# Attention outputs of blocks 2 to 5: one group of TensorE instructions per block instead of two

## The chip, the cores and the metric

The kernel runs on one core of one Trainium2 chip. The metric is device time in microseconds (us) of one execution, lower is better. An execution takes about 234 us. The engines are called as the profile calls them: PE (TensorE matmul), PEld (its weight loads), DVE (VectorE), ACT (ScalarE), POOL (GpSimd), SP (SyncE).

## The reference, cut to what matters

```python
# q, k, v: batch 4, heads 8, sequence 768, head_dim 64; lam: one decay per head
for b in range(nb):                                   # blocks of the sequence
    intra = einsum('bhic,bhjc->bhij', qb, kb) * Dmask      # masked scores
    intra = einsum('bhij,bhjd->bhid', intra, vb)           # scores times v
    inter = einsum('bhid,bhde->bhie', qb * lam_pow, kv_state)   # state product
    out[:, :, sl] = intra + inter
    kv_state = lam_block * kv_state + einsum('bhsd,bhse->bhde', kb_dec, vb)
# x = out as [3072 tokens, 512]
gate = sigmoid(x @ w_gate); val = x @ w_val           # 512 -> 1536
y = (gate * val) @ w_out                              # 1536 -> 512
```

The reference uses blocks of 64 positions. The kernel uses blocks of 128, so six blocks, numbered 0 to 5. In the kernel a block covers 128 positions of all four batches, and its feed-forward part works on 512 tokens at a time.

## The kernel before

The kernel lists the instructions of each engine in an order fixed by hand. Feed-forward work of block n and attention work of block n+1 alternate in the PE stream. These pieces matter here:

```python
ps_at = tile_pool(name="ps_at", bufs=5, space=PSUM)   # scores, outputs, state updates
ps_ff = tile_pool(name="ps_ff", bufs=3, space=PSUM)   # gate, value, projection

def piece_a(n, bs):                    # attention outputs of the batches bs
    for b in bs:                       # state products: 128x128 weights
        OP[n, b] = ps_at.tile([128, HP, C], FP32, name="op", tag="ps")
        for hp in range(HP if n > 0 else 0):
            nc.tensor.matmul(OP[n, b][:, hp, :], lhsT=Sb[:, b, hp, :],
                             rhs=QS[n, b // 2][:, b % 2, hp, :],
                             start=(hp == 0), stop=False, ...)
    for b in bs:                       # score products: 128x64 weights, two column halves
        for hp in range(HP):
            for u in range(2):
                us = slice(u * 64, (u + 1) * 64)
                nc.tensor.matmul(OP[n, b][us, hp, :], lhsT=V[n][:, b, 2 * hp + u, :],
                                 rhs=MT[n, b][:, u, hp, :], ...)
    ...
    for b in bs:                       # output of the attention = input of the feed-forward
        nc.scalar.copy(XT[n][:, :, b, :], OP[n, b])

def a(n, bp):
    piece_a(n, [2 * bp, 2 * bp + 1])   # two batches

    # step n of the loop (n = 2 to 4); block 2 has the same tail, written out before the loop
    gv(n, 0)                           # gate and value matmuls, one slice of d_ff
    c(n, 0)                            # state update, batches 0 and 1
    ...
    sc(nx, 1); m(nx, 1)                # scores of the next block (PE), masked by DVE into MT
    piece_po(n, 1)                     # projection: 12 matmuls of 128x512
    a(nx, 0)
    piece_po(n, 2)
    a(nx, 1)
    piece_po(n, 3)
    # next step begins with gv(nx, 0), which reads XT[nx] of all four batches
```

Per batch the attention output takes 4 state products (full 128x128 weights) and 8 score products (weights of 64 columns, each writing one half of the PSUM partitions). So one group of two batches is 8 state products and 16 score products.

Of the kernel before, what the change touches and what calls it, by code (L numbers as in the profile page):

```python
# [16 lines left out]
def kernel(  # L17
# [13 lines left out]
    B, H, S, D = q.shape  # L31
# [39 lines left out]
    def load(n, what, b0, b1):  # L71
        sl = slice(n * C, (n + 1) * C)
        for c in what:
            lst, src = {"q": (Q, q), "k": (K, k), "v": (V, v)}[c]
            if n not in lst:
                lst[n] = qkv.tile([128, B, H, D], BF16, tag=c + "b", name=c + "b")
            t = lst[n]
            nc.gpsimd.dma_start(  # L78
                out=t[:, b0:b1],
                in_=src[b0:b1, :, sl, :].rearrange("b h s d -> s (b h) d"))  # L80
# [71 lines left out]
    def transpose_by_dma(n):  # L152
        QR[n] = trsb.tile([128, B, HP, C], BF16, tag="QR", name="QR", bufs=2)
        kt = trsb.tile([128, B, HP, C], BF16, tag="KR", name="KR", bufs=2)
        for dst, src in ((QR[n], Q[n]), (kt, K[n])):
            nc.sync.dma_start_transpose(out=dst.rearrange("p b g c -> p (b g) c"),
                                        in_=src.rearrange("p b h d -> p (b h d)"))
        for bp in range(2):
            KS[n, bp] = kt[:, 2 * bp:2 * bp + 2]
# [69 lines left out]
    def piece_a(n, bs):  # L229
        for b in bs:  # L230
# [4 lines that stand above are left out]
                                 start=(hp == 0), stop=False, skip_group_check=True)  # L235
        for b in bs:
# [4 lines that stand above are left out]
                                     rhs=MT[n, b][:, u, hp, :],  # L241
                                     start=(n == 0 and hp == 0), stop=(hp == HP - 1),
                                     skip_group_check=True)
        if n not in XT:
            XT[n] = xtp.tile([128, NMT, B, C], BF16, tag="XT", name="XT")
        for b in bs:
            nc.scalar.copy(XT[n][:, :, b, :], OP[n, b])  # L247
# [12 lines left out]
    def make_kd(n):  # L260
        KD[n] = kdp.tile([128, B, H, D], BF16, tag="kd", name="kd")
        nc.gpsimd.tensor_tensor(  # L262
            out=KD[n], in0=K[n],
            in1=kds.unsqueeze(1).unsqueeze(3).to_broadcast([128, B, H, D]), op=ALU.mult)
# [3 lines left out]
    def fade():  # L268
        for b in range(B):
            SD[b] = kdp.tile([128, HP, 128], FP32, tag="sd", name="sd", bufs=4)  # L270
            nc.gpsimd.tensor_tensor(out=SD[b], in0=Sb[:, b],  # L271
                                    in1=dec.unsqueeze(2).to_broadcast([128, HP, 128]),
                                    op=ALU.mult)
# [54 lines left out]
    def piece_last(n, tt):  # L328
        ob = osb.tile([128, DM], FP32, tag="ob", name="ob")
        for lo, hi in ((0, 384), (384, DM)):  # L330
            po = ps_ff.tile([128, DM], FP32, name="po", tag="ff")
            for ft in range(NFT):
                nc.tensor.matmul(po[:, lo:hi], lhsT=HT[n, ft][:, tt * 128:(tt + 1) * 128],  # L333
                                 rhs=WO[:, ft, lo:hi], start=(ft == 0), stop=(ft == NFT - 1))
            if lo == 0:
                nc.scalar.copy(ob[:, lo:hi], po[:, lo:hi])
            else:
                nc.vector.tensor_copy(ob[:, lo:hi], po[:, lo:hi])
            nc.sync.dma_start(out=out[tt * S + n * C:tt * S + (n + 1) * C, lo:hi], in_=ob[:, lo:hi])

    def piece_po(n, tt):
        po = ps_ff.tile([128, DM], FP32, name="po", tag="ff")
        for ft in range(NFT):
            nc.tensor.matmul(po, lhsT=HT[n, ft][:, tt * 128:(tt + 1) * 128],  # L344
                             rhs=WO[:, ft, :], start=(ft == 0), stop=(ft == NFT - 1))
        ob = osb.tile([128, DM], FP32, tag="ob", name="ob")
        nc.scalar.copy(ob, po)  # L347
        nc.sync.dma_start(out=out[tt * S + n * C:tt * S + (n + 1) * C, :], in_=ob)
# [45 lines left out]
    def c(n, bp):  # L394
        piece_c(n, [2 * bp, 2 * bp + 1])

    def t(n, bp):
        piece_t(n, bp)

    def sc(n, bp):  # L400
        piece_s(n, [2 * bp, 2 * bp + 1])
        piece_m(n, 2 * bp)

    def m(n, bp):
        piece_m(n, 2 * bp + 1)

    def a(n, bp):
        piece_a(n, [2 * bp, 2 * bp + 1])

    def gv(n, *fts):  # L410
        for ft in fts:
            piece_gv(n, ft)
# [48 lines left out]
    sc(2, 1)  # L461
    m(2, 1)
    piece_po(1, 1)
    a(2, 0)
    piece_po(1, 2)
    a(2, 1)
    piece_po(1, 3)
    for n in range(2, NSTEP):
        nx = n + 1
        if nx == NSTEP:  # L470
            gv(n, *range(NFT))
            for tt in range(B - 1):
                piece_po(n, tt)
            piece_last(n, B - 1)
            break
        transpose_by_dma(nx)
        gv(n, 0)
        c(n, 0)
        gv(n, 1)
        c(n, 1)  # L480
        if nx + 1 < NSTEP:
            fade()
            make_kd(nx)
            load(nx + 1, "qkv", 0, B)
        gv(n, 2, 3, 4, 5, 6, 7, 8)
        t(nx, 0)
        gv(n, 9)
        t(nx, 1)
        gv(n, 10)
        sc(nx, 0)  # L490
        gv(n, 11)
        m(nx, 0)
        piece_po(n, 0)
        sc(nx, 1)
        m(nx, 1)
        piece_po(n, 1)
        a(nx, 0)
        piece_po(n, 2)
        a(nx, 1)
        piece_po(n, 3)  # L500


# [28 lines left out]
```

## Time and profile before

| | before |
|---|---|
| time, median of 3 runs | 234.06 us (233.78 to 234.13) |
| span of the profiled run | 231.8 us |
| PE / DVE / ACT / POOL busy | 97% / 46% / 35% / 36% |
| share of PE in the chain that ended last | 91% |
| granted PE clock | full in every slice |

These are lines of the page of the kernel before: its head, the busy times, PE and its granted clock (in tenths, in 40 slices of the span), and the chain of work that ended last.

```profile
span 231.8 us, 3884 instructions
...
PE 224.9 (97%) x1566; PEld 116.1 (50%) x1566; DVE 106.3 (46%) x186; ACT 80.8 (35%) x147; POOL 84.4 (36%) x73
...
PE   7799999999999999999999999999999999999994
...
PEclk9999999999999999999999999999999999999999
...
PE 91%; POOL 6%; issue 1%; ACT 0%; DVE 0%; POOLq 0%
```

PE is the bottleneck, and after the first slices it has no rest. So what leaves the PE stream here should shorten the run, and what PE must wait for should lengthen it. Busy time itself will not show the change, because the ends of matmuls in the profile are modelled and overlap. What one reads is the distance from start to start.

The next lines are the PE instructions of block 4's attention outputs, from the timeline of the kernel before. The columns are start in us, length in us, engine, line, operation, output<-inputs, shape of the weights (rows*columns), and how many instructions are merged in the line.

```profile
154.25 0.61 PE L233 MATMUL op<-QS,Sb 128*128 128x128 bf16 x8
154.79 0.64 PE L240 MATMUL op<-MT,vb 128*64 128x128 bf16 x16
155.36 2.76 PE L344 MATMUL po<-WO,ht 128*128 128x512 bf16 x12
157.96 0.61 PE L233 MATMUL op<-QS,Sb 128*128 128x128 bf16 x8
158.50 0.64 PE L240 MATMUL op<-MT,vb 128*64 128x128 bf16 x16
159.07 2.76 PE L344 MATMUL po<-WO,ht 128*128 128x512 bf16 x12
161.67 0.59 PE L299 MATMUL gp<-XT,WG 128*128 128x512 bf16 x2
```

The shape changes where L233 ends and where L240 ends. From the start of the state products to the start of the score products it is 0.54 us, although eight of them at 56 ns would be 0.45. The score products take 0.57 us, where eight pairs at 56 ns would take 0.45. The single records show where the difference sits: 149 ns from the last state product to the first score product instead of 56; 77 ns to the second pair instead of 53; 152 ns from the last pair to the projection instead of 53; 226 ns after the projection's first matmul instead of 216. These four excesses, 93 + 24 + 99 + 10, add up to 226 ns for one group. From the projection to the state products, both with 128-column weights, it is 216 ns, which is the ordinary step.

### The profile page before, as it was taken

The page shows a single profiled execution, that of the slowest core. Times are in us where ns is not written, and L with a number is a line of the kernel's source. Part 1 is how long each engine was busy: PE and PEld are TensorE (multiplying, and loading weights), DVE is VectorE, ACT ScalarE, POOL GpSimd, SP SyncE. Part 2 cuts the span into 40 slices and gives each one's busy share as a digit, 9 for nine tenths or more (in the row PEclk, how much of TensorE's full clock was granted, in tenths as well). Part 3 has the DMA queues.
Part 4 walks back from the last instruction along what each step waited for, and adds up shares of the span by engine and source line. Part 5 has one row for each costly group of instructions (what it writes and reads, how often), then busy time and mean ns, then how long its engine had stood idle before and what let it go on. Part 6 is the DMA issues. An engine that isn't in the chain of part 4 may idle for free.

```text
span 231.8 us, 3884 instructions
## 1 busy us (share of the span) xinstructions
PE 224.9 (97%) x1566; PEld 116.1 (50%) x1566; DVE 106.3 (46%) x186; ACT 80.8 (35%) x147; POOL 84.4 (36%) x73
## 2 busy tenths in 40 slices
PE   7799999999999999999999999999999999999994
PEld 2444555788544455544455544455544455444442
DVE  4362757554870530845640845840754750243300
ACT  5653343554222224333134243233333223434221
POOL 8999988770596000695000596000000000000000
PEclk9999999999999999999999999999999999999999
DMA  8999999999949992919921919931820012100022
GB/s 57 144 177 174 162 192 158 198 183 156 138 88 120 206 217 75 166 36 134 138 93 45 189 42 113 154 90 53 184 47 0 0 45 93 45 0 0 3 90 91
DMA packets 102465, 24.89 MB, mean 107 GB/s; under 512 B 91568, under 2 KB 99504, under 8 KB 102448
## 3 DMA queue, kind: packets, MB, share of 16 engines
q0 software_dynamic: 82064, 14.16, 83.7%
q1 hardware_dynamic: 20384, 10.49, 20.1%
q8 instruction: 12, 0.20, 0.4%
q14 instruction: 5, 0.04, 0.0%
HBM read 28.32 MB, written 6.29 MB: 149 GB/s over the span
## 4 chain that ended last, share of the span: by engine, by line
PE 91%; POOL 6%; issue 1%; ACT 0%; DVE 0%; POOLq 0%
PE po L344 26%; PE gp L299 24%; PE vp L305 24%; PE vp L322 3%; PE op L240 3%; PE gp L316 3%; PE sp L210 2%; PE op L233 2%; PE cp L279 2%; POOL vb L78 1%; PE po L333 1%; POOL MT L222 1%; POOL qb L78 1%; POOL kb L78 1%; POOL WV L85 1%
## 5 line engine op out<-in xcount | busy, mean ns | idle before, releaser
L308 DVE TENSOR_TENSOR ht<-sg,vp 128x512 bf16<-128x512 bf16 x65 | 44.7, 688 | 85.7 <-PE vp L305 85.4
L305 PE MATMUL vp<-XT,WV 128*128 128x512 bf16 x260 | 66.7, 379 | 0.0
L299 PE MATMUL gp<-XT,WG 128*128 128x512 bf16 x260 | 66.8, 379 | 0.0
L302 ACT ACTIVATE sg<-gp 128x512 bf16<-128x512 f32 x65 | 38.8, 597 | 74.6 <-PE gp L299 74.5
L344 PE MATMUL po<-WO,ht 128*128 128x512 bf16 x276 | 62.6, 380 | 0.0
L344 PEld LDWEIGHTS <-ht 128*128 128x128 bf16 x276 | 25.9, 98 | 30.8
L305 PEld LDWEIGHTS <-WV 128*128 128x128 bf16 x260 | 25.4, 98 | 31.0 <-DMA WV<-in_moe_w_val_dram 0.5
L299 PEld LDWEIGHTS <-WG 128*128 128x128 bf16 x260 | 24.5, 98 | 27.4 <-DMA WG<-in_moe_w_gate_dram 0.4
L271 POOL TENSOR_TENSOR sd<-Sb,dec 128x512 f32<-128x512 bf16 x16 | 16.3, 1038 | 54.0 <-DVE Sb L288 54.0
L227 DVE TENSOR_TENSOR MT<-sp,mask 128x512 bf16<-128x512 f32 x44 | 27.8, 683 | 13.5 <-PE sp L210 13.5
L347 ACT COPY ob<-po 128x512 f32<-128x512 f32 x23 | 13.5, 586 | 52.5 <-PE po L344 48.7
L262 POOL TENSOR_TENSOR kd<-kb,kds 128x2048 bf16<-128x2048 bf16 x5 | 18.1, 3624 | 2.3 <-DMA kb<-in_k_dram 2.3
L247 ACT CAST XT<-op 128x512 bf16<-128x512 f32 x23 | 12.4, 588 | 5.0 <-PE op L240 5.0
L288 DVE TENSOR_TENSOR Sb<-cp,sd 64x256 bf16<-64x256 f32 x32 | 13.5, 420 | 0.8
L78 POOL DMA_DIRECT2D qb<-in_q_dram x9 | 12.4, 1385 | 0.8 <-POOLq L515 0.8
L78 POOL DMA_DIRECT2D vb<-in_v_dram x9 | 12.2, 1360 | 0.0
L78 POOL DMA_DIRECT2D kb<-in_k_dram x8 | 11.5, 1434 | 0.0
L145 PE MATMUL wm<-zero 128*128 128x512 bf16 x26 | 8.9, 477 | 1.2 <-DVE zero L97 1.2
L326 DVE TENSOR_TENSOR ht<-sg,vp 128x256 bf16<-128x256 bf16 x14 | 5.8, 420 | 6.2 <-PE vp L322 3.8
L322 PE MATMUL vp<-XT,WV 128*128 128x256 bf16 x56 | 8.4, 272 | 0.1
L316 PE MATMUL gp<-XT,WG 128*128 128x256 bf16 x56 | 8.4, 273 | 0.0
L240 PE MATMUL op<-MT,vb 128*64 128x128 bf16 x184 | 7.6, 222 | 0.2 <-POOL MT L222 0.2
(62 smaller groups left out, 119.8 us busy)
## 6 DMA issues: line engine op xcount, KB each, us to landing
out_dram<-ob SPq DMA_DIRECT2D x23, 256.0 KB, 2.0
qb<-in_q_dram POOLq DMA_DIRECT2D x4, 512.0 KB, 8.0
kb<-in_k_dram POOLq DMA_DIRECT2D x4, 512.0 KB, 10.0
vb<-in_v_dram POOLq DMA_DIRECT2D x4, 512.0 KB, 13.1
WG<-in_moe_w_gate_dram POOLq DMA_DIRECT2D x6, 256.0 KB, 6.8
WV<-in_moe_w_val_dram POOLq DMA_DIRECT2D x6, 256.0 KB, 7.1
WO<-in_moe_w_out_dram POOLq DMA_DIRECT2D x3, 512.0 KB, 14.2
kb<-in_k_dram POOLq DMA_DIRECT2D x4, 256.0 KB, 6.5
```

Of the source, the lines that this page charges most:

```text
L78: nc.gpsimd.dma_start(out=t[:, b0:b1], in_=src[b0:b1, :, sl, :].rearrange("b h s d -> s (b h) d"))
L227: nc.vector.tensor_tensor(out=MT[n, b][:, u], in0=SP[n, b][u], in1=mask[:, u], op=ALU.mult)
L240: nc.tensor.matmul(OP[n, b][us, hp, :], lhsT=V[n][:, b, 2 * hp + u, :], rhs=MT[n, b][:, u, hp, :], start=(n == 0 and hp == 0), stop=(hp == ...
L262: nc.gpsimd.tensor_tensor(out=KD[n], in0=K[n], in1=kds.unsqueeze(1).unsqueeze(3).to_broadcast([128, B, H, D]), op=ALU.mult)
L271: nc.gpsimd.tensor_tensor(out=SD[b], in0=Sb[:, b], in1=dec.unsqueeze(2).to_broadcast([128, HP, 128]), op=ALU.mult)
L299: nc.tensor.matmul(gp, lhsT=WG[:, mt, fs], rhs=x[:, mt, :], start=(mt == 0), stop=(mt == NMT - 1))
L302: nc.scalar.activation(sg, gp, AF.Sigmoid)
L305: nc.tensor.matmul(vp, lhsT=WV[:, mt, fs], rhs=x[:, mt, :], start=(mt == 0), stop=(mt == NMT - 1))
L308: nc.vector.tensor_mul(HT[n, ft], sg, vp)
L316: nc.tensor.matmul(gp[:, cs], lhsT=WG[:, mt, fs], rhs=x[:, mt, cs], start=(mt == 0), stop=(mt == NMT - 1))
L322: nc.tensor.matmul(vp[:, cs], lhsT=WV[:, mt, fs], rhs=x[:, mt, cs], start=(mt == 0), stop=(mt == NMT - 1))
L344: nc.tensor.matmul(po, lhsT=HT[n, ft][:, tt * 128:(tt + 1) * 128], rhs=WO[:, ft, :], start=(ft == 0), stop=(ft == NFT - 1))
```

## The change

The intent is to compute the outputs of all four batches in one group behind the third projection, so that PE changes its tile shape twice per block for them rather than four times.

```diff
     piece_po(1, 1)
-    a(2, 0)
     piece_po(1, 2)
-    a(2, 1)
+    piece_a(2, range(B))
     piece_po(1, 3)
 ... # and in the loop, for blocks 3 to 5:
         piece_po(n, 1)
-        a(nx, 0)
         piece_po(n, 2)
-        a(nx, 1)
+        piece_a(nx, range(B))
         piece_po(n, 3)
```

The number of instructions of every engine stays the same. Only their order on PE and ACT changes.

## The prediction

> **What bounds the kernel.** TensorE. The page shows PE busy 97% of a 231.8 us span at full granted clock, and the chain that ended last is 91% PE; from 66 us on it is PE without a break. DVE (46%), ACT (35%) and Pool (36%) only have to be in time. So the change is worth what it takes out of the PE stream, unless it makes PE wait.
>
> **What it removes.** No instruction: the instruction order shows the same PE, DVE, ACT, Pool and DMA instructions; each block's first attention-output group moves one projection later, to the second. What goes away is changes of tile shape on PE. A group has state products (128x128 weights), then masked-score products (128x64 weights, two column halves side by side), then PE goes back to 128x128 for the projection. Consecutive PE starts in the timeline at 158 us: inside the state products 56 ns; to the first masked-score matmul 149 (93 more); the first pair takes 77 against 56 (21 more); from the last pair to the projection 152 against 53 (some 97 more); the projection's first matmul 226, not 216 (10 more). Sum about 0.22 us per group; all eight groups of blocks 2 to 5 show these edges. The Trainium skill, "TensorEngine Tiling (Array Packing)", Key Properties, says that a change of tiling mode drains the engine; the trace agrees, with about 95 ns a change. From 512-column matmuls to the state products there is no cost (216 ns). Two groups per block become one: 4 x 0.22 = 0.9 us less. The matmuls themselves cost the same (1.8 us per block).
>
> **Could it add a wait?** I expect none on the path.
> - Masked scores: DVE finishes block 4's last about 154.0 us; the merged group starts about 156.8.
> - PSUM: the merged group holds four output tiles of the pool's five. The rotation of allocations does not change; their previous users are score tiles freed by 154.0 us.
> - XT copies on ACT: four in a row, 0.535 us each, from about 158.3 to 160.5 us. The next gate matmul needs them about 161.4: 1 us slack. State-update tiles, which reuse output tiles, come at 163 us.
> - Projection tiles: three buffers, copied 0.6 us after their end; two projections back to back are no problem.
>
> All 0.9 us lies on the critical path.
>
> **Predicted time.** 234.06 - 0.9 = 233.2 us; 232.8 to 233.7 should hold it 8 times in 10 (runs of before spread 0.35 us). Faster by over 2%: 0.01; within 2%: 0.985; slower by over 2%: 0.005.
>
> **What would show it.** Right: in blocks 2 to 5 one run of 16 state products and one of 32 masked-score products, about 0.9 us each, with one 149 ns and one 152 ns edge; 216 ns between second and third projection; the stretch of projections and outputs 0.22 us shorter per block; the span near 230.9. PE busy time as the page counts it hardly tells, since ends are modelled. Wrong: PE idle or an over-long start before the next block's first gate matmul (ACT's XT copies late) or before the output products (DVE or PSUM), or switches whose cost grows with the group.
>
> **What would make it wrong.** A late XT copy of batch 3 would give back up to 0.2 us a block; another head (the first 60 us depend on loads) can move either way by some 0.2 us.

## The result, and the profile after

| | before | after |
|---|---|---|
| time, median (4 runs each) | 233.99 us | 233.38 us |
| lowest to highest | 233.78 to 234.13 | 233.27 to 233.43 |
| span of the profiled run | 231.8 us | 231.3 us |

The ratio of the change to before is 0.9974, with a 95% interval of 0.9957 to 0.9992. Ratios here are the mean time of one kernel's fast runs over that of the other's of the same rounds, so not quite the ratio of the medians quoted beside them.

These are the lines of the page of the changed kernel that answer to those above.

```profile
span 231.3 us, 3884 instructions
...
PE 224.3 (97%) x1566; PEld 116.1 (50%) x1566; DVE 106.3 (46%) x186; ACT 80.4 (35%) x147; POOL 84.4 (36%) x73
...
PEclk9999999999999999999999999999999999999999
...
PE 90%; POOL 4%; DMA 3%; issue 1%; ACT 0%; DVE 0%; POOLq 0%
```

The page says almost nothing: half a microsecond less, and 3% of the chain now belongs to a DMA, which the change does not touch (a load of w_val in the first 20 us; see "The head"). The timeline of the changed kernel around block 4's outputs says more. It has the same columns, with DVE and ACT shown as well; the bracket at the end is the idle time of the engine before the instruction and what ended it.

```profile
151.50 2.48 DVE L227 TENSOR_TENSOR MT<-sp,mask 128x512 bf16<-128x512 f32 x4 [0.96 <-PE sp L210]
...
151.62 5.35 PE L344 MATMUL po<-WO,ht 128*128 128x512 bf16 x24
...
156.81 1.06 PE L233 MATMUL op<-QS,Sb 128*128 128x128 bf16 x16
...
157.79 1.08 PE L240 MATMUL op<-MT,vb 128*64 128x128 bf16 x32
158.25 2.05 ACT L247 CAST XT<-op 128x512 bf16<-128x512 f32 x4 [0.66 <-PE op L240]
...
158.81 2.76 PE L344 MATMUL po<-WO,ht 128*128 128x512 bf16 x12
...
161.41 1.03 PE L299 MATMUL gp<-XT,WG 128*128 128x512 bf16 x4
```

There is one run of 16 state products and one of 32 score products. Start to start the group takes 158.81 - 156.81 = 2.00 us; the two groups before took 1.11 + 1.11 = 2.22 us. DVE has finished the last masked scores at 153.98 us, long before the group. ACT's four XT copies end at 158.25 + 2.05 = 160.30 us, 1.1 us before the gate matmul that needs them.

Four blocks times 0.22 us is 0.9 us. The profile's span shrank by 0.5 us and the median by 0.6 us. So where is the rest? To see it, the run is cut in two. The **head** goes from the start to the first state-update matmul of block 1, before anything that the change touches. The **body** goes from there to the first matmul of the last, split projection. About 6.1 us of end remain. These two lines per kernel mark the cuts. First those of the timeline of before:

```profile
58.52 0.61 PE L279 MATMUL cp<-vb,kd 128*128 128x128 bf16 x8
...
225.69 0.33 PE L333 MATMUL po<-WO,ht 128*128 128x384 bf16 x1
```

And those of the timeline of the change:

```profile
58.95 0.44 PE L279 MATMUL cp<-vb,kd 128*128 128x128 bf16 x5
...
225.21 0.81 PE L333 MATMUL po<-WO,ht 128*128 128x384 bf16 x4
```

The head is 58.52 us before and 58.95 after, 0.42 us longer (from the unrounded starts). The body is 167.17 us before and 166.26 after, 0.91 us shorter. The expected gain is all there in the body, and the head of this one execution gave back half of it. The instructions of the head are the same in both kernels. Two questions follow: is the body's gain really the shape changes, and is the longer head chance?

### The profile page after: what moved, and what is told of

It reads as the page before. It is cut to its first block, busy times and chain, and to the rows that moved or that the text cites. A ratio compares the mean times of both kernels' runs of the same rounds, so it can differ in the third digit from the quotient of the medians.

```text
span 231.3 us, 3884 instructions
## 1 busy us (share of the span) xinstructions
PE 224.3 (97%) x1566; PEld 116.1 (50%) x1566; DVE 106.3 (46%) x186; ACT 80.4 (35%) x147; POOL 84.4 (36%) x73
## 4 chain that ended last, share of the span: by engine, by line
PE 90%; POOL 4%; DMA 3%; issue 1%; ACT 0%; DVE 0%; POOLq 0%
PE po L344 26%; PE vp L305 24%; PE gp L299 24%; DMA WV<-in_moe_w_val_dram 3%; PE vp L322 3%; PE gp L316 3%; PE sp L210 2%; PE op L240 2%; PE op L233 2%; PE cp L279 2%; PE po L333 1%; POOL qb L78 1%; POOL kb L78 1%; POOL vb L78 1%; PE tk L196 0%
## 5 line engine op out<-in xcount | busy, mean ns | idle before, releaser
L319 ACT ACTIVATE sg<-gp 128x256 bf16<-128x256 f32 x14 | 5.4, 386 | 6.1 <-PE gp L316 4.7
```

## The experiments

The theory: each pair of shape changes (into the score products and out of them) costs PE a fixed 0.226 us, nothing else in the change matters, and the head differs by chance. Three rivals: the gain comes from the new place or from fewer groups, buffers and waits; the cost of a switch depends on how long the group is; the change itself lengthens the head. Eleven further runs were made: eight new kernels, before once more and the change twice more. In the table, head, body and clock are of the one profiled execution of each (the clock is its mean granted share), and time is the median of all its runs. A few profiles lack some 1.5% of the matmul records, which does not touch the cuts.

| kernel | shape changes per block for the outputs | body us | head us | clock | time us | before, same rounds |
|---|---|---|---|---|---|---|
| before | 4 | 167.171 | 58.520 | 1.000 | 233.99 | |
| before_again | 4 | 167.171 | 59.139 | 0.999 | 234.12 | 234.12 |
| two_adjacent | 4 | 167.168 | 59.428 | 0.997 | 233.93 | 234.12 |
| the change | 2 | 166.264 | 58.945 | 1.000 | 233.38 | 233.99 |
| after_again | 2 | 166.263 | 58.978 | 1.000 | 233.29 | 234.12 |
| after_third | 2 | 166.264 | 58.797 | 1.000 | 233.12 | 234.22 |
| mirror | 2 | 166.262 | 59.814 | 0.990 | 233.29 | 234.12 |
| merged_early | 2 | 166.264 | 58.710 | 1.000 | 233.11 | 233.99 |
| four_adjacent | 8 | 168.982 | 59.359 | 1.000 | 236.43 | 233.99 |
| no_switch (wrong result) | 0 | 165.350 | 59.679 | 0.992 | 232.94 | 233.99 |
| merged_last | 2 | 172.384 | 59.145 | 1.000 | 239.53 | 233.99 |
| warm2 | 2 | 166.262 | 60.365 | 0.998 | 233.01 | 234.22 |
| warm4 | 2 | 166.264 | 58.599 | 1.000 | 233.20 | 234.22 |

### Both kernels once more

No edit; 5 rounds each.

> The changed kernel, unaltered. Two parts of the run are measured apart: the head, up to the first state-update matmul of block 1 (58.52 us in the profile of before, 58.95 in that of the change), and the body from there to the last, split projection (167.17 us and 166.26). Theory (tile-shape switches, plus chance in the head): the body is 166.26 within 0.03 again, and the head lands anywhere from about 58.4 to 59.0, so that over more runs the total tends toward 0.9 us under before. Rival (the change itself lengthens the head, by another program layout): the head is again near 58.95, 0.4 over before's, and the time stays 0.5 to 0.6 under before.

> The kernel before, unaltered, for a second profile of its head and the spread between two builds of one kernel. Theory (head varies by chance): body 167.17 within 0.03; head differs from 58.52 by some tenths. Rival (the head is a property of the program): head 58.52 within 0.1. Timed against itself: ratio 1.000 within 0.001.

The bodies came back to within a nanosecond: 166.263 and 167.171 us. The head did not: the kernel before, with head 58.52 the first time, now had 59.14, longer than the change's two. So the head is not a property of the program. (The change's own head, 58.98, would not have told: it is what the rival expected too.) The ratio of before to itself was 1.0004 (0.9990 to 1.0017), that of the change to before 0.9970 (0.9956 to 0.9983).

### Two groups, one straight after the other

```diff
         piece_po(n, 2)
-        piece_a(nx, range(B))
+        a(nx, 0)
+        a(nx, 1)
         piece_po(n, 3)
```

(and the same for block 2)

> Both groups behind the third projection as in the change, but kept as two groups, one after the other: state, scores, state, scores. Theory (the gain is changes of tile shape): four changes per block as before, so the gain is gone: body about 167.1 (0.8 to 0.9 over the change), time like before. Rival (the gain comes from the place, or from running the two groups without a projection between them): body near 166.3.

The body was 167.168 us: the gain is gone, to 3 ns. The time was 233.93 us beside 234.12, ratio 0.9992 (0.9981 to 1.0004). These lines are the PE timeline of this kernel in block 4.

```profile
157.74 0.61 PE L233 MATMUL op<-QS,Sb 128*128 128x128 bf16 x8
158.28 0.64 PE L240 MATMUL op<-MT,vb 128*64 128x128 bf16 x16
158.85 0.62 PE L233 MATMUL op<-QS,Sb 128*128 128x128 bf16 x8
159.40 0.64 PE L240 MATMUL op<-MT,vb 128*64 128x128 bf16 x16
159.97 0.39 PE L344 MATMUL po<-WO,ht 128*128 128x512 bf16 x1
```

The place and the lack of a projection in between do not count. The steps 0.54, 0.57, 0.55 and 0.57 us are the old ones.

### The second group in mirror order

```diff
-        piece_a(nx, range(B))
+        a(nx, 0)                       # state 0,1; scores 0,1
+        piece_a_mirror(nx, [2, 3])     # scores 2,3 (start=(hp == 0)); then state 2,3 (stop)
```

> Two groups one after the other behind the third projection, the second in reverse order: state 0 and 1, scores 0 and 1, scores 2 and 3, state 2 and 3. Same instructions in number, still two groups with two sets of buffers, but only two changes of shape per block. Theory (changes of shape): body as in the change, 166.26 within 0.1. Rival (it is merging the groups that gains, by fewer starts of a group or fewer waits): body near 167.1 as with two groups.

The body was 166.262 us, that of the change, with two groups and two sets of buffers. The PE timeline of this kernel (its line numbers differ: L233 and L260 are state products, L240 and L255 score products):

```profile
157.68 0.61 PE L233 MATMUL op<-QS,Sb 128*128 128x128 bf16 x8
158.22 0.64 PE L240 MATMUL op<-MT,vb 128*64 128x128 bf16 x16
158.69 0.61 PE L255 MATMUL op<-MT,vb 128*64 128x128 bf16 x16
159.23 0.62 PE L260 MATMUL op<-QS,Sb 128*128 128x128 bf16 x8
159.69 0.38 PE L361 MATMUL po<-WO,ht 128*128 128x512 bf16 x1
```

From L240 to L255, another group but the same shape, the step is 0.47 us, with no exit cost; and L260 to the projection, where both have 128 columns, is 0.46 us. Merging as such gains nothing. The changes of shape count, and this pair of runs shows it most cleanly: the same two groups in the same place, with 4 or 2 changes. What in the shape costs is not separated: here 64 columns always come with writing one half of the partitions and with smaller weight loads.

### More switches, and none

```diff
-        piece_a(nx, range(B))          # four_adjacent: one group per batch
+        for b in range(B):
+            piece_a(nx, [b])
```

> Behind the third projection, one group per batch: state, scores, four times over; eight changes of shape per block, against two in the change. If each pair of changes costs a fixed 0.226 us: body (from the first state-update matmul of block 1 to the last projection) 166.26 + 3 x 0.226 x 4 = 168.98 us within 0.1, and about 2.7 us longer than the change in time. If a change's cost grows with the work drained (a group half as long costs half): clearly less, near 168. If nothing hangs on shape: 166.3.

```diff
-                for u in range(2): ... lhsT=V[n][:, b, 2 * hp + u, :], rhs=MT[n, b][:, u, hp, :]
+                # no_switch, blocks 2 to 5: one product with 128 columns, wrong on purpose
+                nc.tensor.matmul(OP[n, b][:, hp, :], lhsT=V[n][:, b, 2 * hp:2 * hp + 2, :],
+                                 rhs=MT[n, b][:, 0, hp, :], start=False, ...)
```

> The change, with the masked-score products of blocks 2 to 5 taken as 16 full 128x128 weights instead of 32 halves of 64 columns (one head of each pair alone: the result is wrong on purpose). 16 full matmuls at 56 ns take what 16 pairs take, so only the two changes of shape per block go. If the switches cost what the edges show: body 166.26 - 4 x 0.226 = 165.36 us within 0.05. If part of the edge belongs to something else, a wait or the start of another accumulation: more than 165.5.

With eight changes the body was 168.982 us (expected 168.98), with none 165.350 (expected 165.36). Each step of the series 0, 2, 4, 8 changes per block, over four blocks, gives the same price for a pair: (166.264 - 165.350) / 4 = 0.229 us, (167.171 - 166.264) / 4 = 0.227, (168.982 - 166.264) / 12 = 0.227. The price does not depend on how long the groups are: in the traces a group of 4 state products (four_adjacent) pays the 149 ns of one with 16. The PE timeline of the kernel without switches (its L239 is the 128-column product, L349 the projection):

```profile
157.09 1.06 PE L233 MATMUL op<-QS,Sb 128*128 128x128 bf16 x16
157.98 1.06 PE L239 MATMUL op<-MT,vb 128*128 128x128 bf16 x16
158.87 0.59 PE L349 MATMUL po<-WO,ht 128*128 128x512 bf16 x2
```

Both steps are 0.89 us, 16 times 56 ns, with bare edges. It is no way out for a correct kernel: 32 full products would take 32 x 56 ns = 1.8 us where the 16 pairs take 0.9.

The times of these two moved a little less neatly than the bodies (236.43 against 233.99, and 232.94 against 233.99), because their heads (59.4 and 59.7 us in the profiles) were among the long ones.

### Where the group may stand

```diff
         piece_po(n, 1)
+        piece_a(nx, range(B))          # merged_early
         piece_po(n, 2)
-        piece_a(nx, range(B))
         piece_po(n, 3)
+        piece_a(nx, range(B))          # merged_last (in its own kernel)
```

> The merged group behind the second projection instead of the third. DVE has the last masked scores about 1 us before they are needed. If only the number of changes of shape counts: body 166.26 within 0.05. If the third place is needed for DVE to be in time: an over-long start before the state or score products, body up to 167.

> The merged group behind the fourth projection, straight before the next gate matmul. Here the four XT copies have no projection to hide behind: the last ends about 2.5 us after the first score product, which is 1.55 us after PE would like to go on. Expected: PE idle about 1.5 us before the first gate matmul in each of four blocks, body about 172.3 us (6 us longer), time 2 to 3% over the change. If ACT's copies were not needed that late, the body would stay at 166.3.

The early group has the same body, 166.264 us: there is room on that side. The late one has 172.384 us and is slower, ratio 1.023 (1.0212 to 1.0247). In its waits of PE (who waited for whom: us in total, times, longest) a new line leads:

```profile
PE gp L299 <- ACT XT L247: 5.9, 4, 1.5
PE wm L145 <- DVE zero L97: 1.2, 1, 1.2
```

The four waits of 1.5 us are ACT's XT copies, which behind the third projection are hidden. So the projection that follows the group is a necessary part of the change; the order of the listing is not indifferent.

### The head

> The change once more, unaltered, to settle how much of the body's 0.908 us arrives in the time, and as the partner of the two runs with filler in this call. Theory (the head varies by chance, whatever the kernel): over this call's runs the mean difference to before lies between 0.6 and 1.2 us; the body is 166.26 again; the head anywhere in 58.5 to 59.9. Rival (the change's head is longer by its program): mean difference near 0.6 or less.

With 5 more rounds the change was at 233.12 us beside 234.22 for before, ratio 0.9952 (0.9937 to 0.9966). Over the three calls with the change, 16 runs of it average 233.29 us and the 26 runs of before in the same calls 234.16: a difference of 0.86 us with a standard error of 0.08, worked out from the scatter of the runs. That agrees with the body's 0.91; the first four runs of each gave 0.61.

The rival, a head made longer by the change, expected a difference of 0.6 or less. The three profiled heads of the change (58.80 to 58.98) lie between the two of before (58.52 and 59.14), which are few; the spans for every run in the calls of after_again and after_third say more. Body and end, taken as in the profiles (166.26 or 167.17 us, and 6.08), leave an estimate of each run's head: on average 59.0 us for the 12 runs of the change and 59.0 for the 22 of before (58.7 to 59.7 and 58.4 to 59.6). A head longer by 0.4 us is not there.

What makes the head wander? Two things are visible. One is when loads land. The traces of before and of the change show most of their 0.42 us there: from the last matmul of the first gate group to the first value matmul, which waits for the first slice of w_val, it is 420 ns in before and 682 in the change, but 676 in before_again as well. PE also waits near 10.5 us for the second half of block 0's k, until 10.6 us in before and until 11.2 to 11.4 us in two_adjacent, mirror, four_adjacent and no_switch. The other is the granted clock. These windows (stretch in us; its length; busy time of PE, PEld, DVE, ACT, POOL with counts; granted clock; DMA share; GB/s) are of mirror:

```profile
10.00:12.00 2.00, 1.03 (x18) 0.68 (x16) 1.29 (x2) 0.67 (x3) 2.00 (x4) 1.00 2.43 155
12.00:14.00 2.00, 1.69 (x10) 0.95 (x11) 1.02 (x2) 1.03 (x2) 2.00 (x3) 0.67 2.42 154
14.00:16.00 2.00, 2.00 (x20) 1.07 (x19) 1.66 (x4) 0.59 (x1) 1.23 (x2) 0.50 1.73 185
```

And these of two_adjacent, whose load came just as late:

```profile
10.00:12.00 2.00, 1.08 (x20) 0.67 (x16) 1.29 (x2) 0.69 (x2) 2.00 (x4) 1.00 2.44 156
12.00:14.00 2.00, 1.62 (x18) 0.94 (x20) 1.24 (x3) 1.07 (x2) 2.00 (x3) 1.00 2.41 156
14.00:16.00 2.00, 1.81 (x30) 1.02 (x28) 1.93 (x4) 0.85 (x2) 1.96 (x3) 1.00 1.70 186
```

With PE about equally busy from 10 to 12 us, the clock fell to half in one execution and not in the other; the first gate matmul came at 18.67 us in mirror and 17.62 in two_adjacent.

The Trainium skill, "TensorE: Matmul & The Clock Gate", What's actually happening, describes a window that runs freely, not started by the kernel, and decides on the clock. In no_switch the clock fell the same way (0.61 and 0.53 in the same two windows), and the clock records of the traces fit such a window. In both runs there is one stretch at half clock of 3.41 us (from 12.70 us in mirror, from 12.45 in no_switch) after 6.83 us at full clock, and the full stretches of all thirteen profiles are whole multiples of 3.41 us. Cut on that grid, the stretch before the dip had PE busy 55% in both, and the one that holds the same wait 61% and 60% in two_adjacent and four_adjacent, which kept the full clock. So where a wait falls on the grid may decide; but warm2 had a stretch of 54% (16.51 to 19.93 us) and kept the clock, so no limit is shown.

The last two runs tried to prevent the dip on top of the change, with extra matmuls on zeros in the wait.

```diff
     piece_m2(0, 1, 0)
+    idle(2)        # warm2; idle(4) in warm4
     piece_tk0(1)
```

> The change, with two more filler matmuls on zeros where PE waits near 10.5 us for the second half of the first k block. In two of ten profiles that wait was long (to 11.2 and 11.3 us) and the granted clock fell to about half from 12 to 16 us, which moved the first gate matmul from 17.2-17.7 to 18.5-18.7 us. If filler prevents it: body 166.26, head at most 59.4, no run over 233.7 us in time, median 0.1 to 0.2 us under the change. If the clock falls for another reason: some runs over 233.9 as before. Cost where the load is early: none, as the first gate matmul waits for other work.

> The same with four filler matmuls (0.86 us at full clock): surer against the clock, but it ends at 11.3 us, later than the load in most profiles. Expected: body 166.26, no run over 233.8 us; median within 0.15 us of that with two, as the first gate matmul at 17.2 us hides up to 0.4 us of delay. If PE's own work before it is the limit: median 0.3 to 0.5 us longer.

The outcome is inconclusive. In both profiles the clock stayed full in those windows, but it also had in nine of the eleven profiles without the extra matmuls. Five of six runs of warm2 took 232.80 to 233.22 us and the sixth, the profiled one, 234.74; there PE waited 1.70 us for the first w_val slice, as one line of its PE timeline shows:

```profile
20.07 1.04 PE L305 MATMUL vp<-XT,WV 128*128 128x512 bf16 x4 [1.70 <-DMA WV<-in_moe_w_val_dram]
```

The medians of warm2 and warm4 (233.01 and 233.20 us) cannot be told from the change's (233.12), and warm2's expectations of no run over 233.7 us and of a head of at most 59.4 (it was 60.37) were misses, as were warm4's of none over 233.8 (one took 234.18) and of a median within 0.15 us of warm2's (0.19). Their premise, that the long wait for k brings the dip, was only half true: two_adjacent and four_adjacent had that wait too and kept the clock. No version that beats the change was shown.

## Why the prediction was right

The prediction named 233.2 us, with 232.8 to 233.7 as range; the measured median was 233.38 us, and 233.29 and 233.12 later. Point by point:

- **PE is the limit, so what leaves its stream leaves the time.** Right. In the body, PE starts follow each other without a wait, and the saving goes through undiminished to the last projection.
- **What goes away is shape changes, 0.22 us per group and 0.9 us in all.** Right, and shown: 0.227 us per pair, 0.907 us in the body. The two_adjacent and mirror kernels separate the changes of shape from merging and from place, and the series 0, 2, 4, 8 gives their price three times over. The prediction's 0.22 was summed from edges in one trace, and the sum of edges held. (It took 77 ns against 56 and 97 for 99; with the ordinary step of 53 in both places the sum is 0.226.)
- **The page cited from the skill.** "TensorEngine Tiling (Array Packing)", Key Properties, says that a change of mode drains the engine. The page has no size for it; the runs do. That the extra time is a drain is the page's word. The prediction's "the trace agrees" holds for the cost, some 95 ns a change, and not for the drain: the trace shows only that the time hangs on the change of shape.
- **No new wait.** Right. DVE was done 2.8 us before the group. ACT's copies ended at 160.30 us (predicted about 160.5) and the next gate matmul started at 161.41 us (predicted about 161.4). The merged_last kernel shows that this was a real condition: without the projection behind the group the same copies cost 1.5 us per block.
- **The head may move either way by some 0.2 us.** The mechanism was right and its size was off. Heads ran from 58.52 to 60.37 us over thirteen profiles, ten of the others within 58.6 and 59.7. The profile of before that the prediction was built on happened to have the shortest. That is why the profiled span came out at 231.3 us where 230.9 was predicted. Why the first four runs of each showed 0.6 us of the 0.9 is not shown, since the spans of those runs of before are not on record; the later calls gave 0.83 and 1.10 between medians.

## What to carry to other kernels

On a kernel bound by PE, read start-to-start distances at the edges of each group of matmuls: a step that is longer than its neighbours where only the shape of the weights changes is a cost that reordering can remove, here 0.227 us per pair of changes. In the trace of the change one more such pair stands twice per block, untouched and untried: the score products of the next block (64x128 weights), 312 ns on entry from a 512-column matmul instead of 216, and 148 instead of 53 on exit. Before gathering such groups, check what each consumer of their results has to hide behind, because the same merged group one projection later made the body 6.1 us longer. And when the gain is smaller than the wander of the run, cut the trace at a point before the change and at one after it: here the parts repeated to a few ns while the totals scattered by half a microsecond and more.

## What the Trainium skill lacked or had wrong

- "TensorEngine Tiling (Array Packing)", Key Properties, says that a mode switch drains the engine, without a size. Here, from 128x128 to 128x64 weights and back: 149 ns instead of 56 on entry, 77 instead of 53 at the second pair, 152 instead of 53 on exit, 226 instead of 216 at the next matmul; 0.227 us for the pair of changes, whether the group has 4 state products or 16.
- "TensorE: Matmul & The Clock Gate", Back-to-back issue gap, gives sustained rates in a real kernel of about 81 ns per matmul at 128 moving columns and 131 ns at 512, and sets 56 and 216 ns apart as the isolated case. In this kernel, with a weight load for every matmul, the sustained steps at full clock were 56 and 216 ns away from changes of shape.
- The same page, in Why this matters for your kernels, advises against PE idle gaps over about 3 us because an idle window lowers the clock. In mirror the granted clock fell to 0.50 for 3.41 us though the longest single wait before it was 0.80 us, with PE busy 55% of the 3.41 us before; in merged_last four waits of 1.5 us in an otherwise full stream left it at full. No page says how busy a window must be to keep the clock, and 54% in warm2 kept it.
